# Gated mix of a state-space convolution and a shift-MLP on one core: whole first loads in another order, and the last token tile in two column pieces

## The chip, the cores and the metric

The kernel runs on one core of a Trainium2 chip. A core has a matrix engine (PE), which multiplies a stationary 128 x 128 block of weights with a moving block of up to 512 columns into a bank of PSUM; a vector engine (DVE); a scalar engine (ACT); GpSimd (POOL); and a sync engine (SP). SP and ACT also issue the transfers (DMAs) between main memory and the core's own memory. Each engine takes its instructions in program order and waits on semaphores. The metric is the device time of one execution in microseconds; lower is better.

## What is computed

Cut from the reference (one sequence of 2048 tokens with 448 channels, 1792 hidden channels):

```python
x = A_u
g = sigmoid((x * gate_w).sum(-1, keepdims=True))
a = A_ref(x, ...)                    # diagonal state-space convolution over the tokens, plus x * D_skip
h = gelu(layernorm(x) @ w1)          # 448 x 448
hs = concat([h0 shifted +1, h1 shifted -1, h2 shifted +2, h3 shifted -2]) @ w2   # four groups of 112 channels
x1 = x + hs
b = x1 + gelu(layernorm(x1) @ w3) @ w4    # 448 x 1792, 1792 x 448
return g * a + (1 - g) * b
```

## The kernel before

The tokens are worked in 4 blocks of 512, each block as 4 token tiles of 128. The work of PE is cut into units. A unit ("a", b, g) is the product of block b with one group g of the columns of w1, then its shift and gelu, then its part of the product with w2; a unit ("d", b, f) is the same for 128 hidden channels of w3 and w4. Each unit has a first product (`first`, L463, into a bank `p`: weights in the array, 512 tokens moving) and a second product (`second`, L583, into four banks `acc0` to `acc3`, one per token tile). The units of a block come in the group order 0, 2, 1, 3. Group 2 is smaller than the others: 64 columns of w1 instead of 128.

Full precision is kept by splitting: an operand is rounded by ACT to a high part (`xh`, `w1h`, `uh`, in a reduced float format) and DVE subtracts it from the original to get the low part (`xl`, `w1l`, `ul`). A product is then three products, high by high, high by low and low by high. For group 2 the high and the low columns stand side by side in one tile, `w1d`.

The layer norm ahead of w1 is folded into the weights and the output: PE computes the column means of a group of w1 (`col_means`, L851, and `presum_mean` for group 0, L900, with a constant `cm` of 1/448 as the stationary operand, into a bank `pm`), DVE subtracts them (`center`, L905), and the reciprocal deviation of each token is multiplied in later (rows turned by PE through `rows_of`, L362, then `rb`).

The first block is started piece by piece. The loads are issued by `first_loads` (L255): the three or four transfers that matter first are on two queues, ACT's and SP's, where each queue's transfers are issued in order. `w1r` holds w1 in four column groups, `raw` holds the transposed first block of x as a left half (`x0[:, :4*HW]`, in two transfers: contraction tiles 0 and 1, then 2 and 3) and a right half (L278), `xs` holds tokens by rows, `raw<-xb` are the later blocks of x.

While loads are under way, PE runs warm-up products (`warm_up`, L889): a constant tile of bf16 against itself into a bank that nobody reads, 512 columns each. The tile `warm` is set to zero by POOL (L286).

The order of the first block's steps is the string `ORDER` (L1057 to L1072), which `begin` (L1086) walks word by word. `w` is one warm-up; `m0` to `m3` the column means of a group; `c` centering; `h` and `l` high and low parts of w1; `wh`, `wl` the same for w2; `xha`, `xhb`, `xla`, `xlb` high and low parts of the left (a) and right (b) half of x; `sa`, `sb`, `ra` statistics of the tokens; `p1:h1a` a first product of unit 1 with high weights, contraction tile 1, left half; `s0:21` a second product of unit 0. The words fix the order on every engine, since all are recorded in this order. From unit 6 on, a loop over the units sets the order.

At the end, `last_two` (L619) does the second products of the last two units tile by tile: for each of four token tiles six products of 448 columns, then on DVE the add `xs = acc * gs + xs` (L631), then the output transfer of that tile (`done`, L575). `done` issues the transfer when both the convolution's part and the MLP's part of a tile are in; for the first three blocks this happens in the middle of the kernel, as the convolution's results come in.

Of the kernel before, what the change touches and what calls it, by code (L numbers as in the profile page):

```python
# [179 lines left out]
def mixer_and_small_steps(ctx, tc, xs, gg, okm, x, xT, xb, x0, w1, w2, w3, w4, gate, par, logdt, dskip, ident, out):  # L180
# [74 lines left out]
    def first_loads():  # L255
# [16 lines left out]
        act(xs[:, 0, :], x[0:128])  # L272
# [12 lines left out]
    def constants():  # L285
        nc.gpsimd.memset(warm[:, :TB], 0.0)  # L286
        nc.gpsimd.memset(cm[:, 0:1], 1.0 / D)
        nc.gpsimd.memset(cm[:64, 1:2], 1.0 / D)
# [286 lines left out]
    def done(b, j):  # L575
        q = NT * b + j
        parts[q] = parts.get(q, 0) + 1
        if parts[q] == 2:
            nc.sync.dma_start(out[q * 128:(q + 1) * 128], xs[:, q, :])

    ADDED = {}

    def second(n, only=None):  # L583
# [10 lines left out]
        for j, p in only or q:  # L594
            first_, last_ = s and p == 0, e and p == 2
            if only:
# [22 lines left out]
    def last_two():  # L619

        n = len(units) - 2
        for j in range(NT):
            t = slice(j * 128, (j + 1) * 128)
            for m in (n, n + 1):
                wh, wl = W4[units[m][2]]
                for p in range(3):
                    nc.tensor.matmul(ACC[j], (UL if p == 2 else UH)[m][:, t], wl if p == 1 else wh,  # L627
                                     start=False, stop=m > n and p == 2)
            q = NT * (NB - 1) + j
            r = xs[:, q, :]  # L630
            nc.vector.scalar_tensor_tensor(r, ACC[j], gs[:, q:q + 1], r, op0=OP.mult, op1=OP.add)  # L631
            done(NB - 1, j)

# [255 lines left out]
    def warm_up(m):  # L889
        for _ in range(m):  # L890
            nc.tensor.matmul(pw, warm[:, 0:128], warm[:, :TB], start=True, stop=True)  # L891

# [164 lines left out]
    ORDER = """  # L1057
    ws xha m0 xla m2 c0 sk xha xz xz c0 h0 w h0 l0 p0:h1a sa0 m1 c2 l0 h2 sa0 p0:h2a l2 p0:l0a w c1 p0:l2a
    p1:h2a sa1 p1:x1a p0:x0a ld m3 xla h1 xla p1:x0a sa1 p1:x2a sb3 p0:x1a p2:h0a,x1a p0:x2a,l1a c3 p0:l3a
    sa2 p1:h1a,h0a p2:x2a p0:h3a sb3 p2:h3a l1 p2:x0a xhb pe sb3 h3 p0:h0a p1:h3a p0:l1b p2:h1a p1:h0b xlb  # L1060
    xhb p2:h1b,l1b p1:h1b p3:x0a sa2 p3:h0b l3 p2:l3a p1:h2b p2:l0b p1:x1b p0:h0b sb3 p0:h2b wh0 xlb
    p3:l2b,x0b p0:x1b ra0 p0:l2b,x0b ra0 p2:x1b xlb p0:h1b p3:h0a,h3a ra0 xh1 p1:x2b ra0 p3:l3a p0:x2b ra0
    p0:h3b p3:h1a ra0 xh1 p1:x0b ra0 p3:h2a,l3b ra0 p1:h3b xh1 p0:l0b ra0 p3:h1b sk p0:l3b p3:l2a wl0 p3:l0a
    xh1 ra sk uf0 p3:l1a sk p2:x0b xl1 p3:x2b p2:h2b uf1 p3:h3b p2:l1a mu0 sk p4:l0 mu0 p2:h2a sk p4:h2 ad1
    hd0 p3:x2a p2:l0a,h3b p4:l3 hd0 mu0 mu1 p3:l0b rm mu1 p3:l1b hd0 p2:l2a p5:h0 hd0 p2:l3b xl1 s0:00 ba
    p2:x2b p4:h0,h3 hd0 xl1 p5:h2 bm p5:h1 hd0 xl1 p4:x0 wh2 p2:l2b p3:x1b s0:10 tl0 hd0 s0:20 wh1 p2:h0b
    tl0 p4:h1 s0:11 hd1 sb7 p3:h2b s0:12 p5:h3 wh3 mu2 p3:x1a s0:30 cp1 p5:x0 wl2 p5:x1,x2 hd2 s0:32 tl1
    s0:22 p4:l2 hd2 hd2 p4:x2 sb5 p4:l1 s1:21 sb7 cp2 mu3 s1:01 s0:31 p4:x1 tl2 s2:20 s0:02 s1:11 sb5 s0:21
    sb7 hd3 s2:10 s0:01 s1:20 sb5 cp2 hd3 s2:32 hd3 s1:00 sb7 s1:30 sb5 s2:30 ra1 cp3 wl1 s2:22,00,02 uf5
    ra1 s1:10 ra1 s3:10 ra1 cp3 s2:11 ra1 wl3 s1:31 s2:21,01 ra1 s3:20 ra1 s3:30 ra1 s2:31 ra1 s3:21 tl3 rn  # L1070
    ad5 s3:31 bn s3:00,11,01,22 mu4 s3:12,32,02 sb9 hd4 s2:12 re hd4 hd4 re cp4 mu5 cp4 sb9 tl4 hd5 re cp5
    re  # L1072
    """
# [12 lines left out]
    def begin():  # L1086
# [4 lines left out]
        hl_tiles(("a", 1))  # L1091
        warm_up(8)
        for word in ORDER.split():
# [175 lines left out]
```

## Time and profile before

| | us |
|---|---|
| median of 3 runs | 375.67 (375.15 to 375.73) |
| the profiled execution | 374.8 |
| span of that execution, first to last instruction | 372.9 |
| PE busy | 364.2 |
| DVE busy | 307.0 |
| ACT busy | 215.7 |
| POOL busy | 64.4 |
| mean granted clock of PE | 0.992 of full |

The span is what the trace covers; some 1.9 us of the execution lie around it. "PEld" in the views is the loading of weights into the array, which runs beside PE's products. The chain of waits is followed back from the last instruction, each step to what released it. In a row of the timeline the columns are start, length, engine, line, operation, output and inputs, shape, count, and in brackets the idle time before and what ended it. In a row of a table of windows they are, after the window and its length, the busy time and count of PE, PEld, DVE, ACT and POOL, then the granted clock, the share of the DMA engines that was busy, and the rate in GB/s. In a row of DMA issues they are the queue, the count, the size, and the time from issue to landing.

### The profile page before, as it was taken

What the parts mean: (1) busy time and instruction counts of PE and PEld (TensorE: products, weight loads), DVE (VectorE), ACT (ScalarE), POOL (GpSimd) and SP (SyncE); (2) the same over time, 40 slices, a digit from 0 to 9 for tenths busy, and PEclk for the clock granted to TensorE, in tenths of its full rate; (3) what the DMA queues carried; (4) which work ended last, traced back from release to release, by engine and by line L of the source; (5) the groups of instructions that cost most, each with busy time, mean ns of one, the idle gap of its engine ahead of it and who ended that gap; (6) DMA issues with size and microseconds to landing.
All of it is one profiled execution on the core that took longest, in us unless ns stands there. A gap on an engine that the chain in (4) does not pass through costs nothing.

```text
span 372.9 us, 5290 instructions
## 1 busy us (share of the span) xinstructions
PE 364.2 (98%) x1730; PEld 315.5 (85%) x1730; DVE 307.0 (82%) x565; ACT 215.7 (58%) x382; POOL 64.4 (17%) x177
## 2 busy tenths in 40 slices
PE   6999999999999999999999999999999999999994
PEld 3998888888888888888888888888888888888883
DVE  1899979787989997468789899998789999999422
ACT  2985759678493636945174674554756645445220
POOL 2000340200220000030023324224243324000000
PEclk9899999999999999999999999999999999999998
DMA  7995024635949055001743613457375611361212
GB/s 214 388 395 194 2 99 90 123 113 201 386 139 247 11 101 168 0 0 50 141 141 70 94 29 85 121 174 128 74 135 113 177 22 22 78 177 30 67 46 104
DMA packets 88175, 46.14 MB, mean 124 GB/s; under 512 B 67152, under 2 KB 82512, under 8 KB 87504
## 3 DMA queue, kind: packets, MB, share of 16 engines
q1 hardware_dynamic: 87696, 45.14, 44.3%
q10 hardware_dynamic: 448, 0.62, 0.6%
q8 instruction: 15, 0.25, 0.3%
q14 instruction: 16, 0.13, 0.1%
HBM read 34.74 MB, written 11.01 MB: 123 GB/s over the span
## 4 chain that ended last, share of the span: by engine, by line
PE 97%; DMA 2%; ACTq 0%; DVE 0%; issue 0%
PE p L480 48%; PE acc L602 45%; DMA w1r<-w_in 2%; PE acc L627 1%; PE pm L855 1%; PE misc L365 0%; DVE xs L631 0%; PE pw L891 0%; ACTq L269 0%; ACTq L267 0%; PE pe L833 0%; PE misc L723 0%
## 5 line engine op out<-in xcount | busy, mean ns | idle before, releaser
L541 ACT ACTIVATE uf<-p 128x512 f32<-128x512 f32 x56 | 33.5, 597 | 113.1 <-PE p L480 113.0
L480 PE MATMUL p<-xh,w3l 128*128 128x512 f32 x224 | 70.1, 395 | 0.0
L480 PE MATMUL p<-xh,w3h 128*128 128x512 f32 x224 | 70.0, 394 | 0.0
L746 DVE TENSOR_TENSOR_SCAN z<-z,carry 128x512 f32<-128x512 f32 x48 | 61.6, 1282 | 3.9
L602 PE MATMUL acc<-w4l,uh 128*128 128x448 f32 x216 | 56.3, 367 | 0.0
L602 PE MATMUL acc<-w4h,uh 128*128 128x448 f32 x216 | 56.0, 365 | 0.0
L602 PE MATMUL acc<-w4h,ul 128*128 128x448 f32 x216 | 55.9, 365 | 0.0
L571 DVE TENSOR_TENSOR ul<-uf,uh 128x512 fp32r<-128x512 f32 x56 | 38.2, 681 | 20.0 <-ACT uh L551 19.7
L480 PEld LDWEIGHTS p<-xh,w3l 128*128 128x128 f32 x224 | 42.1, 188 | 9.8
L480 PE MATMUL p<-xl,w3h 128*128 128x512 f32 x168 | 47.7, 392 | 0.0
L480 PEld LDWEIGHTS p<-xh,w3h 128*128 128x128 f32 x224 | 42.2, 188 | 6.6
L602 PEld LDWEIGHTS acc<-w4h,uh 128*128 128x128 f32 x216 | 40.5, 188 | 6.0
L602 PEld LDWEIGHTS acc<-w4h,ul 128*128 128x128 f32 x216 | 40.6, 188 | 3.5
L602 PEld LDWEIGHTS acc<-w4l,uh 128*128 128x128 f32 x216 | 40.6, 188 | 3.4
L741 ACT ACTIVATE z<-zs,nu 128x512 f32<-128x512 f32 x64 | 42.3, 709 | 0.0
L480 PEld LDWEIGHTS p<-xl,w3h 128*128 128x128 f32 x168 | 31.5, 188 | 7.2
L551 ACT ACTIVATE uh<-uf 128x512 fp32r<-128x512 f32 x56 | 35.4, 633 | 1.8
L740 POOL COPY z<-carry 128x1 f32<-128x1 f32 x48 | 32.5, 688 | 16.0 <-DVE zs L752 15.9
L748 POOL COPY carry<-z 128x1 f32<-128x1 f32 x48 | 13.5, 282 | 104.5 <-DVE z L746 103.2
L346 POOL TENSOR_TENSOR t<-r 128x4 f32<-128x4 f32 (+1 forms) x5 | 3.1, 626 | 118.1 <-DVE r L345 118.1
L746 DVE TENSOR_TENSOR_SCAN z<-z,carry,zero 128x512 f32<-128x512 f32 x16 | 20.0, 1248 | 0.0
L602 PE MATMUL acc<-w2h,uh 128*128 128x448 f32 x64 | 19.7, 367 | 0.0
(195 smaller groups left out, 540.2 us busy)
## 6 DMA issues: line engine op xcount, KB each, us to landing
zs<-xT_in SPq DMA_DIRECT2D x4, 1024.0 KB, 7.8
yd<-yt SPq DMA_DIRECT2D x56, 64.0 KB, 2.0
ysb<-yd SPq DMA_DIRECT2D x16, 224.0 KB, 2.7
out_dram<-xs SPq DMA_DIRECT2D x16, 224.0 KB, 2.9
raw<-xb_in SPq DMA_DIRECT2D x3, 1032.0 KB, 12.6
raw<-w_in SPq DMA_DIRECT2D x3, 1024.0 KB, 5.7
xd<-xt SPq DMA_DIRECT2D x16, 192.0 KB, 2.1
xr<-xd SPq DMA_DIRECT2D x16, 192.0 KB, 3.1
```

The costliest lines, as they stand in the source:

```text
L346: eng.tensor_mul(t, y, y)
L480: nc.tensor.matmul(p[:, t0:t1], (wl if w else wh)[:, k, :], (xl if x_ else xh)[:, k, o + t0:o + t1], start=(q == 0 and fresh), stop=stop i ...
L541: nc.scalar.activation(UF[n], P1[n], AF.Gelu_apprx_tanh)
L551: nc.scalar.activation(UH[n], UF[n], AF.Copy)
L571: nc.vector.tensor_sub(UL[n], uf, f32(UH[n]))
L602: nc.tensor.matmul(ACC[j], (UL if p == 2 else UH)[n][:, t], wl if p == 1 else wh, start=first_, stop=last_)
L627: nc.tensor.matmul(ACC[j], (UL if p == 2 else UH)[m][:, t], wl if p == 1 else wh, start=False, stop=m > n and p == 2)
L740: nc.gpsimd.tensor_copy(z4[:, m, 0:1], carry[:, k, m:m + 1])
L741: nc.scalar.activation(z4[:, m, 1:], ZS[b][:, k, :], AF.Copy, scale=nu[:, k, m:m + 1])
L746: nc.vector.tensor_tensor_scan(z, z, up, carry[:, k, m:m + 1], OP.add, OP.add)
L748: nc.gpsimd.tensor_copy(carry[:, k, m:m + 1], z[:, TB - 1:])
L855: nc.tensor.matmul(p, cm[:, c:c + 1].to_broadcast([128, 128]), W1R[g][:, k, :], start=k == 0, stop=k == 3)
```

## The change

Four things change.

The first loads. Before, group 0 of w1 and the first transfer of x were each issued in two pieces of 64 rows, one on ACT's and one on SP's queue, and group 2 of w1 came third on ACT's. Now group 2 is first on ACT's queue and group 0 second; x's left half is first and second on SP's; all in pieces of 128 rows. The rest follows in the order of before.

The warm-ups use a bf16 constant 1.0, broadcast, that exists before the kernel's own instructions start; the tile `warm` and its memset go. Six warm-ups stand ahead of the table's first word instead of eight, and six words `w` of it instead of two.

The table `ORDER` has another order of the same steps of the first block, for all engines.

The last token tile. Its bank `acc3`, with all units but the last two, is added to `xs` at the start of `last_two`. The last two units' products for that tile go to two banks of their own, of 320 and 128 columns, each with its own add and its own transfer. Also, the first block's four output transfers go in two pieces of 64 rows each.

The diff, without most of the table:

```diff
-    warm = big.tile([128, 2 * TB], mybir.dt.bfloat16, name="warm", tag="yt")
+    warm = nc.const_aps.tensor(1.0, [128, TB], mybir.dt.bfloat16)
...
-        for q, p in ((act, slice(0, 64)), (sp, slice(64, 128))):
-            q(w1r[p, :512], w1[p, :512])
-        for q, p in ((act, slice(0, 64)), (sp, slice(64, 128))):
-            q(r[p, :2 * HW], x0[p, :2 * HW])
         load_w1(act, 2)
+        sp(r[:, :2 * HW], x0[:, :2 * HW])
+        load_w1(act, 0)
         sp(r[:, 2 * HW:4 * HW], x0[:, 2 * HW:4 * HW])
         act(xs[:, 0, :], x[0:128])
         load_w1(sp, 1)
...
-        nc.gpsimd.memset(warm[:, :TB], 0.0)
...
         if parts[q] == 2:
-            nc.sync.dma_start(out[q * 128:(q + 1) * 128], xs[:, q, :])
+            for p in range(0, 128, 64 if b == 0 else 128):
+                t = slice(p, p + (64 if b == 0 else 128))
+                nc.sync.dma_start(out[q * 128 + t.start:q * 128 + t.stop], xs[t, q, :])
...
-            first_, last_ = s and p == 0, e and p == 2
+            first_, last_ = s and p == 0, (e or n == len(units) - 3 and j == NT - 1) and p == 2
...
         n = len(units) - 2
+        last = NT * NB - 1
+
+        def add(acc, q, c):
+            r = xs[:, q, c]
+            nc.vector.scalar_tensor_tensor(r, acc, gs[:, q:q + 1], r, op0=OP.mult, op1=OP.add)
+
+        add(ACC[NT - 1], last, slice(0, D))
         for j in range(NT):
             t = slice(j * 128, (j + 1) * 128)
-            for m in (n, n + 1):
-                wh, wl = W4[units[m][2]]
-                for p in range(3):
-                    nc.tensor.matmul(ACC[j], (UL if p == 2 else UH)[m][:, t], wl if p == 1 else wh,
-                                     start=False, stop=m > n and p == 2)
             q = NT * (NB - 1) + j
-            r = xs[:, q, :]
-            nc.vector.scalar_tensor_tensor(r, ACC[j], gs[:, q:q + 1], r, op0=OP.mult, op1=OP.add)
-            done(NB - 1, j)
+            for c in (slice(0, D),) if q < last else (slice(0, D - 128), slice(D - 128, D)):
+                acc = ACC[j] if q < last else ps.tile([128, c.stop - c.start], F32, name="p1", tag="p1", bufs=3)
+                for m in (n, n + 1):
+                    wh, wl = W4[units[m][2]]
+                    for p in range(3):
+                        nc.tensor.matmul(acc, (UL if p == 2 else UH)[m][:, t], (wl if p == 1 else wh)[:, c],
+                                         start=q == last and m == n and p == 0, stop=m > n and p == 2)
+                add(acc, q, c)
+                if q < last:
+                    done(NB - 1, j)
+                else:
+                    nc.sync.dma_start(out[q * 128:(q + 1) * 128, c], xs[:, q, c])
...
-            nc.tensor.matmul(pw, warm[:, 0:128], warm[:, :TB], start=True, stop=True)
+            nc.tensor.matmul(pw, warm[:, 0:128], warm, start=True, stop=True)
...
-        ws=each((presum,)), m0=each((presum_mean,)), w=each((warm_up, 1), (warm_up, 1), (warm_up, 1), (warm_up, 1)),
+        ws=each((presum,)), m0=each((presum_mean,)), w=each(*((warm_up, 1) for _ in range(6))),
...
-    ws xha m0 xla m2 c0 sk xha xz xz c0 h0 w h0 l0 p0:h1a sa0 m1 c2 l0 h2 sa0 p0:h2a l2 p0:l0a w c1 p0:l2a
+    w m2 xha ws w c2 m0 xla h2 xz xha w l2 sk sa0 xz c0 p1:h1a c0 p1:h0a,x0a h0 m1 xla h0 l0 sa0 w c1 p1:x1a
...
-        warm_up(8)
+        warm_up(6)
```

The order of instructions, at three places. First, PE at its first column means; `pm` with 64 columns is group 2, with `ws` group 0, the next `pm` group 1; `p` is a bank of a first product, with `w1d` that of group 2. Before:

```order
L891 MATMUL pw<-warm 128x512
L903 MATMUL pm<-w1r,cm 128x128 x2
L903 MATMUL pm<-ws,cm 128x128
L855 MATMUL pm<-w1r,cm 128x64 x4
L891 LDWEIGHTS warm
L891 MATMUL pw<-warm 128x512
L480 MATMUL p_175<-xh,w1h 128x256
L855 MATMUL pm<-w1r,cm 128x128 x4
```

and now:

```order
L901 MATMUL pw<-const-bfloat16-1.0 128x512
L865 MATMUL pm<-w1r,cm 128x64 x4
L901 LDWEIGHTS const-bfloat16-1.0
L901 MATMUL pw<-const-bfloat16-1.0 128x512
L913 MATMUL pm<-w1r,cm 128x128 x2
L913 MATMUL pm<-ws,cm 128x128
L901 LDWEIGHTS const-bfloat16-1.0
L901 MATMUL pw<-const-bfloat16-1.0 128x512
L477 MATMUL p_172<-xh,w1d 128x256 x2
L477 MATMUL p_172<-xl,w1d 128x256
L865 MATMUL pm<-w1r,cm 128x128 x4
```

The means of group 2 have moved ahead of those of group 0, and three products of group 2's unit stand ahead of the means of group 1, where one of unit 0 stood.

Second, ACT's first rows: its transfers, and the load of its function table. Before:

```order
L267 DMA w1r<-w_in 64x512
L269 DMA raw<-x_in 64x520
L264 DMA w1r<-w_in 128x256
L272 DMA xs<-x_in 128x448
L1089 ACT_TABLE_LOAD
```

and now:

```order
L264 DMA w1r<-w_in 128x256
L264 DMA w1r<-w_in 128x512
L270 DMA xs<-x_in 128x448
L1098 ACT_TABLE_LOAD
L1098 ACTIVATE rt<-cm 128x1
```

The transfer of 128 x 256 is group 2; it was third and is first, and group 0 (128 x 512), whose first 64 rows were first here, is second as a whole.

Third, the same engine where the second block of x (`raw`, 128x516) is copied and unit 0's bank is taken. Before:

```order
L910 ACTIVATE w2h<-w2r 128x448
L396 ACTIVATE xh<-raw 128x516 x4
L966 ACTIVATE uf<-p_175 128x512
L491 ACTIVATE uf<-p_194 64x512
L990 ACTIVATE ug<-uf 128x256
L993 ACTIVATE ug<-uf 16x255
```

and now:

```order
L920 ACTIVATE w2h<-w2r 128x448
L393 ACTIVATE xh<-raw 128x516 x4
L976 ACTIVATE uf<-p_190 128x512
L488 ACTIVATE uf<-p_172 64x512
L1000 ACTIVATE ug<-uf 128x256
L920 ACTIVATE w2h<-w2r 128x448
L1003 ACTIVATE ug<-uf 16x255
```

The rows up to the first gelu (`ug`) stand in the same order; one copy of w2 now stands ahead of the next.

More of the change, by code (lines that the diff above doesn't have):

```diff
@@ L1063, in mixer_and_small_steps @@
[L1063 to L1072, printed above, removed]
+    w m2 xha ws w c2 m0 xla h2 xz xha w l2 sk sa0 xz c0 p1:h1a c0 p1:h0a,x0a h0 m1 xla h0 l0 sa0 w c1 p1:x1a
@@ new lines, in mixer_and_small_steps @@
+    p0:h0a,x1a,l1a,h2a xla h1 w ld m3 l0 sa1 l1 p1:h2a sa2 p1:x2a c3 p0:h3a p2:h0a w p2:l2a sb3 p1:h3a h3
+    p0:x0a p2:h3a pe sb3 xhb sb3 p0:h1a,x2a,l0a xhb p0:l3a xlb p2:x1a p0:l1b,l2a p1:h0b sa2 p2:x0a p3:h2a
+    xlb p2:x2a p0:h1b p3:x2a sb3 xlb p2:l3a sa1 p1:x2b p2:l0b l3 p2:h1b p1:h2b p0:l3b,l2b p3:x2b wh0 p1:x1b
+    ra0 p3:h1b p2:x1b ra0 p2:h2b ra0 p1:h3b p2:h3b ra0 p0:h0b xh1 p1:h1b ra0 p0:x0b ra0 p2:x0b,l0a ra0
+    p1:x0b xh1 p0:l0b ra0 p2:h2a ra0 p0:x1b wl0 p0:h2b xh1 p0:h3b p2:h0b p0:x2b p3:h0a sk p2:l1a xh1 p3:l2a
@@ new lines, in mixer_and_small_steps @@
+    sk p3:x1a sk ra uf0 xl1 p3:x0a,x1b,l3b uf1 p3:h3a mu0 p2:h1a sk mu0 p2:l3b p4:l1 sk mu0 rm hd0 p2:x2b
+    p3:h0b ad1 wh2 p3:h3b p4:l0 p2:l2b p4:h1 hd0 sb7 mu1 p3:h2b,l2b hd0 p5:h3 mu1 p4:h2 hd0 p4:l2 s0:10 tl0
+    hd0 p3:h1a,l0b xl1 ba p3:l1a,x0b p2:l1b s0:00 bm s0:02 wl2 hd0 p5:h2 hd0 p5:h0 hd1 sb5 p3:l0a p5:h1
+    s0:30 wh1 tl0 s0:31 p3:l3a sb5 cp1 s0:12 mu2 p5:x0 p4:h0 sb7 s0:20 tl1 hd2 s0:22 p4:x0 s0:32 sb5 hd2
+    s0:21 hd2 p3:l1b s1:01 sb7 s0:11 cp2 p4:h3 xl1 s1:10 p4:l3 wh3 s0:01 sb5 s1:30 sb7 tl2 s1:11,20 p5:x1
@@ L1073, in mixer_and_small_steps @@
+    ra1 s2:10 mu3 s2:20,22,12 ra1 wl1 hd3 s2:32 s1:31 s2:30 ra1 s2:00 hd3 ra1 hd3 xl1 p4:x1 s2:01 s1:21 cp3
+    ra1 s2:11 ra1 s2:21 ra1 s2:31 cp2 ra1 cp3 p5:x2 tl3 p4:x2 uf5 s1:00 s3:20 ra1 wl3 s3:00 s2:02 s3:32 sb9
+    rn ad5 s3:21 bn s3:12,01,11,22 mu4 s3:31,02,10 mu5 hd4 s3:30 re hd4 hd4 re cp4 re hd5 tl4 cp4 cp5 re sb9
     """
```

4 lines of the change are left out of this document (removed).

## The prediction

> **What bounds the kernel now.** I read the page's first and fourth parts, then the chain in order of time, then the windows of the first 14 us.
>
> ```profile
> PE 364.2 (98%) x1730; PEld 315.5 (85%) x1730; DVE 307.0 (82%) x565; ACT 215.7 (58%) x382; POOL 64.4 (17%) x177
> PE 97%; DMA 2%; ACTq 0%; DVE 0%; issue 0%
> ```
>
> PE is 97% of the chain that ended last, and DMA is the only other share that counts. The chain says where:
>
> ```profile
> 1.98 5.83 DMA w1r<-w_in
> ...
> 7.84 1.62 PE pm L855 x8
> ...
> 10.25 1.63 PE pm L855 x8
> ...
> 12.82 0.89 PE pm L855 x8
> 13.71 1.66 PE p L480 x14
> ...
> 37.13 2.53 PE p L480 x11
> ...
> 357.89 2.55 PE p L480 x11
> ...
> 362.88 4.91 PE acc L627 x24
> 367.79 0.02 issue
> 367.81 0.68 DVE xs L631
> ```
>
> Columns: start, length, what. From 7.84 to 367.8 every piece is PE's. The block of 11 products takes 2.53 us at 37 and 2.55 at 358: the middle is a dense, even beat that the change leaves alone. Time can be won or lost only before 37.13, where that beat begins, and after 362.9. The only wait ahead is for 64 columns of w1 (group 2, issued at 1.98, landed at 7.81). The three groups of column means show a second loss: 8 matmuls take 1.62 us on 64 columns and 1.63 on 128, but 0.89 at 12.82. The windows say why:
>
> ```profile
> 4.00:6.00 2.00, 1.60 (x9) 1.05 (x6) 0.29 (x1) 0.57 (x2) 0.19 (x1) 1.00 0.64 158
> 6.00:8.00 2.00, 0.15 (x1) 0.16 (x2) 0.00 (x0) 0.62 (x1) 0.00 (x0) 1.00 1.00 357
> 8.00:10.00 2.00, 2.00 (x10) 1.63 (x11) 1.71 (x5) 1.34 (x5) 0.31 (x2) 0.56 1.04 386
> 10.00:12.00 2.00, 2.00 (x12) 1.95 (x12) 1.25 (x5) 2.00 (x7) 0.00 (x0) 0.58 1.01 359
> ```
>
> The last three columns are granted clock, DMA share and GB/s. PE did 0.15 us of work from 6 to 8, and the clock then fell to 0.56 and 0.58: some 3.4 us at half speed between 8 and 12. The DMA column shows a sag: 158 GB/s from 4 to 6, 357 and more after.
>
> **Part 1: the first loads and the order.** Group 2 goes from third place on ACT's queue to first, group 0 from first on both queues to second on ACT's, the left half of x0 from second on both to first on SP's. The bytes ahead of group 1 and of everything later are the same; two issues fewer stand ahead on SP and ACT together. So I price it by three later gates, each a thing on which PE must wait in either order, at the landings of before.
>
> ```profile
> 2.91 0.43 SPq L264 DMA_DIRECT2D w1r<-w_in  x1
> 4.75 0.83 SPq L264 DMA_DIRECT2D w1r<-w_in  x1
> 9.52 0.44 SPq L236 DMA_DIRECT2D raw<-xb_in  x1
> w1r<-w_in SPq DMA_DIRECT2D x1, 256.0 KB, 6.5
> raw<-xb_in SPq DMA_DIRECT2D x1, 1032.0 KB, 7.5
> 17.07 2.19 ACT L396 ACTIVATE xh<-raw 128x516 fp32r<-128x516 f32 x4
> 20.34 0.60 ACT L966 ACTIVATE uf<-p 128x512 f32<-128x512 f32 x1 [1.07 <-PE p L480]
> ```
>
> The fourth row answers for both w1 issues, each asked alone: landed 2.91 + 6.5 = 9.4 (group 1) and 4.75 + 6.5 = 11.25 (group 3).
>
> Gate 1, the means of group 1. Before, they ran at 10.25 to 11.88, late because the means of group 2, a warm-up and a product stood ahead at half clock. In the new order the means of groups 2 and 0 and three products stand ahead, whose loads are issued first, so I let these means start on their load, 9.4, at full clock: done at 9.4 + 0.9 = 10.3, or 1.58 earlier. Behind them the new order has three warm-ups for one and two products fewer: a product of 256 columns is 1.66/14 = 0.119, a warm-up of 512 twice that, so 2 x 0.23 - 2 x 0.12 = 0.22. Worth 1.36.
>
> Gate 2, the means of group 3: earliest 11.25, done at 12.14 instead of 13.71, or 1.57; one warm-up more and one product fewer behind: 1.46. From 13.71 to 37.13 the chain has no gap, so PE has no other slack there.
>
> Gate 3, ACT. It copies the second block of x at 17.07, as its load lands (9.52 + 7.5 = 17.0), until 19.26, and then waits 1.07 us for PE's first unit. If PE is earlier, that wait shrinks, and after 1.07 us ACT is the late one: its copy feeds the gelu of unit 0 and PE's second products. ACT's new order has the same rows there. So at unchanged landings the head gains the least of the three, **1.07 us**.
>
> All three gates move if landings do. Without the sag, 2 us x (371 - 158) = 426 KB more would have moved, 1.1 us at 386 GB/s. Nothing in the diff plainly ends it: two queues still ask for the same bytes from the start, only the 64-row pieces go. I take 0.3 of 0 to 1.1: head **1.4 us**, between 0 (last rival but one) and 2.2.
>
> Beside this: the memset of the warm tile goes, so the warm-ups may start before 1.31.
>
> ```profile
> 1.31 3.60 PE L891 MATMUL pw<-warm 128*128 128x512 bf16 x8 [1.31 <-POOL cm L288]
> ```
>
> Seven at 3.60/8 = 0.45 us are 3.2 us; begun by 1.31 they end by 4.5, fill a wait, and cost nothing unless group 2 lands before that. The output of the first block in halves puts four more issues of about 0.4 us on SP past the middle; PE's beat there asks nothing of them.
>
> **Part 2: the last tile.** The bank of the last tile is added early, an add of 0.68 us on DVE while PE still does the first of the four tiles: covered. Then 6 matmuls of 320 columns and 6 of 128 take the place of 6 of 448.
>
> ```profile
> 366.08 2.77 SPq L579 DMA_DIRECT2D out_dram<-xs  x3
> 366.40 0.36 PE L627 MATMUL acc<-w4h,uh 128*128 128x448 f32 x1
> 367.21 0.19 PEld L627 LDWEIGHTS acc<-w4h,ul 128*128 128x128 f32 x1
> 367.42 0.36 PE L627 MATMUL acc<-w4h,ul 128*128 128x448 f32 x1
> L907 DVE TENSOR_TENSOR w1r<-w1r,pm 128x256 f32<-128x256 f32 x3 | 1.2, 415 | 0.0
> 4.13 0.29 DVE L898 TENSOR_TENSOR ws<-w1r 128x128 f32<-128x128 f32 x1 [4.13 <-DMA w1r<-w_in]
> out_dram<-xs SPq DMA_DIRECT2D x1, 224.0 KB, 2.0
> out_dram<-xs SPq DMA_DIRECT2D x1, 224.0 KB, 2.8
> yd<-yt SPq DMA_DIRECT2D x56, 64.0 KB, 2.0
> ```
>
> One of 448 columns takes 4.91/24 = 0.205, one of 256 takes 0.119, so one of 320 takes 0.148. The first piece ends at 366.40 + 5 x 0.148 + 0.30 = 367.44; its add lasts 0.50 (between 0.415 for 256 and 0.68 for 448): 367.97. The second piece starts at 367.29. No row has 128 columns in this format. Below: half of 256, 0.06. Above: a weight load's 0.19. I take 0.11, the means' 0.89/8, the nearest row in columns. Then PE ends at 368.1, the add of 0.29 at 368.42 instead of 368.49. The gain is 0.07; with 0.06 it is 0.2, with 0.19 a loss of 0.4. SP issues the first piece at 368.0, 0.33 each by the last row of three (368.85 - 368.52), so it is free for the second.
>
> Landing: the last transfer of 224 KB took 2.8, the one before 2.0, so 0.8 of it is not size; 64 KB elsewhere took 2.0. The two pieces send the same bytes over the same engines 0.4 us apart, so I take 2.6 of 2.0 to 2.8. Tail: 0.07 + 0.2 = **0.27 us**, between -0.4 and +1.0.
>
> **Sum.** 1.4 + 0.27 = 1.67 us. The profiled span becomes 372.9 - 1.7 = 371.2, its execution 374.8 - 1.7 = 373.1. The median of the shown runs, 375.67, is 0.9 above that execution; I take the difference from the median: **374.0 us**.
>
> **Rivals.**
>
> *The sag goes* (chance 0.18). For it: fewer, whole pieces. Against: queues and bytes are the same. Head 2.2, tail 0.4: 373.0.
>
> *A half-speed stretch all the same* (0.15). PE may be idle twice, before the means of group 0 and of group 1. If 8 to 11 is granted half, the means of group 1 take 1.63, and products and warm-ups up to those of group 3 double: the latter end 0.6 later, 1.46 becomes 0.86, and with the tail 1.1: 374.6. [...]
>
> *Slower* (0.12): group 0 comes too late. PE takes its means in order ahead of nearly all products. Group 0 now stands second on ACT's queue. First, it had landed by 4.13, as DVE's add shows; third there, a load landed at 9.0:
>
> ```profile
> 2.62 0.44 ACTq L272 DMA_DIRECT2D xs<-x_in  x1
> xs<-x_in ACTq DMA_DIRECT2D x1, 224.0 KB, 6.4
> ```
>
> If it lands at L and the clock is half, its means take about 1.0, a warm-up 0.43, three products 0.6, the means of group 1 1.63: done at L + 3.7, plus the 0.22 of gate 1. Against 11.88 that breaks even at L = 8.0. At 9.0 the head loses 1.05, the whole 0.8: 376.5. Against it: the loads that now stand ahead of its landing (groups 2 and 0, the first of x0's left half) were the first to land before too, all by 7.81, which is just under 8.0.
>
> *The head's gain is hidden* (0.10): DVE, 1.71 us of 2 busy from 8 to 10, or the right half of x0 is the late one, and PE starts early only to wait later. Only the tail is left: 375.4.
>
> **How the numbers follow.** The forecast has 0.45. What a measurement tells from no change is 0.2%, 0.75 us: 374.9 and 376.4. Faster: 0.40 of the forecast, 0.18, and 0.09 of the half-speed case, 0.67. Same: the rest of these, 0.11, and the hidden case, 0.10: 0.21. Slower: 0.12. The range goes from 372.7 (head 2.2, tail 0.8) to 376.2, short of most of the slow case; the forecast's own is 373.3 to 374.8 (landings 0 to 0.9 earlier with the tail's smaller ends).
>
> **What would show it.** Right: the means of group 2 begin by 4 or 5 and no longer wait for the last load; means of group 1 done by 10.3 and of group 3 by 12.2; the beat that began at 37.13 begins at about 35.7; ACT's copy of unit 0 no longer waits for PE; the last add ends near 367.0. Wrong: a wait for group 0 beyond 8, clock under 0.7 around 8 to 12, a new wait on PE between 14 and 36, or a second piece whose matmuls stand 0.19 apart.

## The result: 373.17 us, faster by 0.7%

| | before | changed |
|---|---|---|
| median, 11 runs each | 375.33 (374.14 to 377.69) | 373.17 (372.26 to 374.36) |
| profiled execution / its span | 374.8 / 372.9 | 373.1 / 371.3 |

The ratio is 0.9932, 95% interval 0.9914 to 0.995: a gain of 2.6 us (1.9 to 3.2) of 375.33. The medians differ by 2.2 and the two profiled executions by 1.7 (spans 1.6). The forecast was 374.0 and 1.67. The three measures of one gain disagree because one execution of either kernel differs from the next by about as much as the change is worth (spans of the changed kernel run from 370.5 to 372.6); why is taken up below.

The chain of waits of the changed kernel, in order of time (start, length, what):

```profile
0.73 3.69 DMA w1r<-w_in
4.42 0.14 issue
4.55 1.94 PE pm L865 x8
6.49 0.43 PE pw L901
...
6.92 1.65 PE pm L913 x6
8.57 0.43 PE pw L901
9.00 0.64 PE p L477 x3
9.64 1.08 PE pm L865 x8
10.72 0.22 PE pw L901
...
11.78 0.89 PE pm L865 x8
12.67 1.18 PE p L477 x8
...
36.43 2.52 PE p L477 x11
...
362.15 3.68 PE acc L636 x18
365.82 1.51 PE p L636 x12
```

The wait for the first group of w1 now ends at 4.42 instead of 7.80, and from 4.55 on the chain is PE alone. The means of group 1 are done at 10.72 (before 11.88), those of group 3 at 12.67 (13.71). The even beat of 11 products begins at 36.43 instead of 37.13, 0.70 earlier. The last 24 products start at 362.15 instead of 362.88, so the middle takes 325.72 against 325.75 and is unchanged. From there to the end of the span it is 9.2 instead of 10.05. So the profiled pair has 0.7 in the head and 0.9 in the tail, where 1.4 and 0.27 were forecast.

PE began the means of group 2 3.3 us earlier, and its beat came only 0.7 earlier. Part of that is the order: before, the means of group 0 were done by 5.6, while PE waited for group 2; now they stand behind. The rest is the clock, as the same rows show: the 8 means of group 2 take 1.94, a warm-up 0.43, the means of group 0 1.65. These are durations at half speed; the later groups of 8 at full speed take 0.89 and a warm-up 0.22. Full speed comes within the means of group 1 (9.64, 1.08). The windows of the changed kernel (busy time of PE, PEld, DVE, ACT and POOL, granted clock, DMA share, GB/s):

```profile
4.00:6.00 2.00, 1.45 (x7) 1.48 (x8) 0.00 (x0) 0.64 (x1) 0.00 (x0) 1.00 0.91 267
6.00:8.00 2.00, 2.00 (x9) 1.41 (x9) 1.10 (x3) 0.44 (x2) 0.19 (x1) 1.00 1.04 394
8.00:10.00 2.00, 2.00 (x10) 1.78 (x10) 1.86 (x6) 2.00 (x6) 0.33 (x2) 1.00 1.06 406
```

The clock column says 1.00 from the start although the durations halve only near 9.9: it knows a clock only from the first change that the trace recorded, here at 9.9. Ahead of that, durations must be read. The last column shows the other half: 267 GB/s from 4 to 6 us, where the kernel before had 158. The sag is gone, and all landings moved. For groups 1 and 3 of w1, SP's issues in the changed kernel and, behind them, the time from each issue to its landing:

```profile
1.65 0.43 SPq L264 DMA_DIRECT2D w1r<-w_in  x1
4.43 0.33 SPq L264 DMA_DIRECT2D w1r<-w_in  x1
...
w1r<-w_in SPq DMA_DIRECT2D x1, 256.0 KB, 6.4
...
w1r<-w_in SPq DMA_DIRECT2D x1, 256.0 KB, 5.5
```

Group 1 landed at 1.65 + 6.4 = 8.1 instead of 9.4, group 3 at 4.43 + 5.5 = 9.9 instead of 11.25: 1.3 earlier. The two do it in different ways. Before, SP took 0.59, 0.83 and 0.61 us to issue the three pieces ahead of group 1; now it takes 0.40 and 0.42 for two. So group 1 was issued at 1.65 instead of 2.91, and by these rows that is all of its gain, for from issue to landing it took 6.4, much as before (6.5). Group 3 was issued only 0.3 earlier, but took 5.5 instead of 6.5.

The tail, from the timeline of the changed kernel (PE, DVE, SP's queue) and, behind it, the row of its last DMA issue (KB, us from issue to landing):

```profile
365.66 0.30 PE L636 MATMUL p<-w4h,uh 128*128 128x320 f32 x1
365.80 0.31 PE L636 MATMUL p<-w4l,uh 128*128 128x320 f32 x1
...
366.93 0.28 PE L636 MATMUL p<-w4l,uh 128*128 128x128 f32 x1
367.05 0.28 PE L636 MATMUL p<-w4h,ul 128*128 128x128 f32 x1
...
366.74 0.97 DVE L625 SCALAR_TENSOR_TENSOR xs<-p,gs,xs 128x320 f32<-128x320 f32 x2 [0.19 <-PE p L636]
...
367.32 0.85 SPq L642 DMA_DIRECT2D out_dram<-xs  x2
```

```profile
out_dram<-xs SPq DMA_DIRECT2D x1, 64.0 KB, 2.2
```

Products of 320 columns stand 0.145 apart on average, those of 128 0.11. The last add ends at 367.71, 5.56 after the start of the last 24 products; before it was 5.61. The last transfer, issued at 367.74, landed 2.2 later instead of 2.8, and the span ended 1.4 after that landing instead of 1.6.

### The profile page after: what moved, and what is told of

The parts are those of the page before. It is cut to its first block, busy times and chain, and to the rows that moved or that the text cites. A ratio compares the mean times of both kernels' runs of the same rounds, so it can differ in the third digit from the quotient of the medians.

```text
span 371.3 us, 5308 instructions
## 1 busy us (share of the span) xinstructions
PE 365.9 (99%) x1737; PEld 316.7 (85%) x1738; DVE 307.7 (83%) x567; ACT 215.7 (58%) x382; POOL 64.7 (17%) x176
## 4 chain that ended last, share of the span: by engine, by line
PE 98%; DMA 1%; DVE 0%; issue 0%
PE p L477 49%; PE acc L601 45%; PE pm L865 1%; DMA w1r<-w_in 1%; PE acc L636 1%; PE misc L362 0%; PE pm L913 0%; PE p L636 0%; PE pw L901 0%; DVE xs L625 0%; PE pe L843 0%; PE misc L733 0%
## 5 line engine op out<-in xcount | busy, mean ns | idle before, releaser
L750 POOL COPY z<-carry 128x1 f32<-128x1 f32 x48 | 33.7, 714 | 16.0 <-DVE zs L762 15.9
L601 PE MATMUL acc<-w2l,uh 128*128 128x448 f32 x64 | 19.7, 369 | 0.0
```

What stands on the lines that cost most here:

```text
L601: nc.tensor.matmul(ACC[j], (UL if p == 2 else UH)[n][:, t], wl if p == 1 else wh, start=first_, stop=last_)
L750: nc.gpsimd.tensor_copy(z4[:, m, 0:1], carry[:, k, m:m + 1])
```

## The experiments

They ran on three chips: 1 to 4, 5 to 8 and 9 to 12. The kernel before ran beside them on each (medians 376.23, 376.36 and 376.99). "Full from" is where the granted clock, or the durations, reach full speed for good.

**1. The new last tile alone** (e1_tail): the kernel before with the new `last_two`, the early add and its stop flag.

```
-            first_, last_ = s and p == 0, e and p == 2
+            first_, last_ = s and p == 0, (e or n == len(units) - 3 and j == NT - 1) and p == 2
...
+            for c in (slice(0, D),) if q < last else (slice(0, D - 128), slice(D - 128, D)):
```

> The kernel before, with the new last token tile alone (two pieces, early add), and nothing else of the change. Theory: the tail is worth what the two profiles show from the first of the last 24 products to the end, 10.05 us before and 9.15 after: 0.9 us less, of which some 0.2 hang on where the last transfer's semaphore stands in SP's closing list and may be missing here, so 0.6 to 0.9 us faster than before. Rival (the prediction's size): 0.27. Second rival: the last landing was late by chance in the one profile, and the tail is worth 0.1 or less. The first products should stay as before (beat from about 37.1).

Measured: 375.2, ratio 0.9976 (0.9955 to 0.9997), so 0.9 us with an interval of 0.1 to 1.7. The tail is worth more than 0.27, though the interval takes that in.

**2. Everything but the new last tile** (e2_head): the changed kernel with the old `last_two`.

```
-            first_, last_ = s and p == 0, (e or n == len(units) - 3 and j == NT - 1) and p == 2
+            first_, last_ = s and p == 0, e and p == 2
...
-        add(ACC[NT - 1], last, slice(0, D))
```

> The changed kernel with the old last tile (four tiles of 448 columns, one add and one transfer each). Theory: all but the tail's 0.6 to 0.9 us stays: 1.5 to 2.0 us faster than before. Rival: head and tail do not add, because an earlier head only brings the same waits later: under 0.8 faster. In the profile the beat of 11 products should begin near 36.4, as in the changed kernel.

Measured: 374.81, ratio 0.9965 (0.9949 to 0.9981), so 1.3 us (0.7 to 1.9). This is less than the theory's 1.5 to 2.0, though the interval takes that in; it is the forecast's 1.4, and not the 0.70 of the profiled pair. Yet in its own profiled execution PE reaches full speed only at 11.9, and the beat begins at 37.16, where 36.4 was expected, and later than the 37.13 of the kernel before.

**3. Whole outputs of the first block** (e3_nohalves).

```
-            for p in range(0, 128, 64 if b == 0 else 128):
-                t = slice(p, p + (64 if b == 0 else 128))
-                nc.sync.dma_start(out[q * 128 + t.start:q * 128 + t.stop], xs[t, q, :])
+            nc.sync.dma_start(out[q * 128:(q + 1) * 128], xs[:, q, :])
```

> The changed kernel, with the first block's four output transfers whole again: four transfers fewer in the middle. Theory: transfers take their eight semaphores in turn, so the last transfer's semaphore moves four places ahead in the list that SP waits for at the end; four more waits of about 0.07 us stand behind the last landing: 0.2 to 0.3 us longer from last landing to end (1.38 to about 1.65), hardly to be seen in the time. Rival: SP's four issues fewer, of 0.4 each, are worth something in the middle: faster than the changed kernel by 0.5 or more.

Measured: 373.74, ratio 0.9928 (0.9901 to 0.9955). The time does not tell it from the changed kernel. In the traces, the time from the last landing to the end of the span is 1.69 here, and 1.41 in seven of the eight profiles that have both the halves and the new tail (the eighth, experiment 6, has 1.85). The transfers take their semaphores in turn (in the two profiles of the pair eight semaphores, one after the other, for 213 and 216 transfers), so four more of them shift which one the last transfer gets. Over all fourteen profiles the stretch goes by that semaphore, as the trace numbers them: 1.85 us with 102 (experiment 6), 1.77 with 103, 1.69 with 104 (experiments 3 and 9), 1.62 with 105 (the kernel before), 1.54 with 106 (experiment 1), 1.48 with 108 and 1.41 with 110, or 0.06 to 0.08 less from each to the next. So it follows from how many transfers the program has. That SP waits for the semaphores one after the other as it closes the program is inferred from the trace.

**4. Eight warm-ups for six** (e4_warm8).

```
-        warm_up(6)
+        warm_up(8)
```

> The changed kernel with eight warm-up products at the start for six (nine with the table's first one). Theory: in its profile PE stands idle from 3.9 to 4.5, and PE runs at half speed until 9.9: 8 column means of group 2 take 1.94 us, the 6 of group 0 take 1.65. With nine warm-ups of 0.43 PE is busy without a gap from 0.77 to 4.65, and full speed may come one window (3.4 us) earlier: the column means of group 0 then in about 0.7 to 0.9, those of group 1 done by 9.5 for 10.7; up to 1 us faster than the changed kernel, if the loads then leave PE work. Rival: when full speed comes is a matter of phase and not of the gap; then 0.2 us slower, since group 2 waits for the warm-ups.

Measured: 373.07, ratio 0.9913 (0.9891 to 0.9935); full from 5.1; means of group 1 done at 10.29, of group 3 at 12.24, beat at 36.00. The seven warm-ups of the changed kernel last 3.15 us, nine last 4.0. This profile and that of experiment 2 have the same phase of the clock against the program (changes at 5.13 and 11.92 are 2 x 3.41 apart, less 0.04): with the gap filled PE is granted full speed at 5.1, without at 11.9, and the beat begins 1.16 earlier, though group 0 landed 0.37 later. The theory's grant came, but the means of group 1 were done at 10.29 and not by 9.5: PE now waited for group 0, which landed at 7.13. The time does not tell this kernel from the changed one.

**5. The old order of work with the new loads** (e5_oldorder).

```
-    w m2 xha ws w c2 m0 xla h2 xz xha w l2 sk sa0 xz c0 p1:h1a c0 p1:h0a,x0a h0 m1 xla h0 l0 sa0 w c1 p1:x1a
+    ws xha m0 xla m2 c0 sk xha xz xz c0 h0 w h0 l0 p0:h1a sa0 m1 c2 l0 h2 sa0 p0:h2a l2 p0:l0a w c1 p0:l2a
...
```

> The changed kernel with the order of work of the kernel before (new loads, new tail kept). Theory A (loads and order belong together): the old order takes the means of group 0 first, and group 0 now lands second, at about 6.9 instead of 4.1; PE begins at 6.9, 2.4 us later than the change, and the beat of 11 products that began at 36.43 begins at 37.0 to 37.6; only the tail is left, ratio 0.995 to 0.998. Rival B (the earlier landings of groups 1 and 3 are what pays, whatever the order): beat at 36.2 to 36.7, ratio 0.992 to 0.9945.

Measured: 374.58, ratio 0.9951 (0.9933 to 0.9969): the low end of theory A, and 1.8 us where the tail alone gave 0.9. The profiled execution was the slowest of its seven (span 373.4, median 372.7): PE stood idle from the end of its six warm-ups at 3.5 to 7.18, it was at half speed until 13.7, the beat began at 38.44, 0.8 later than A allowed. Neither theory is settled by it; B's early beat is not seen.

**6. The old loads with the new order of work** (e6_oldloads).

```
-        load_w1(act, 2)
-        sp(r[:, :2 * HW], x0[:, :2 * HW])
-        load_w1(act, 0)
+        for q, p in ((act, slice(0, 64)), (sp, slice(64, 128))):
+            q(w1r[p, :512], w1[p, :512])
+        for q, p in ((act, slice(0, 64)), (sp, slice(64, 128))):
+            q(r[p, :2 * HW], x0[p, :2 * HW])
+        load_w1(act, 2)
```

> The changed kernel with the split first loads of the kernel before (new order, new tail kept). Theory A: the means of group 2 come first but group 2 lands third, at 7.8; PE starts on them there with nothing done before, where the kernel before had the means of group 0 done; beat at 37.3 to 38.3, the sag of 158 GB/s from 4 to 6 us is back, groups 1 and 3 land at 9.4 and 11.2; ratio 0.996 to 1.0. Rival B (order of the work alone pays): beat at 36.2 to 36.7, ratio 0.992 to 0.9945.

Measured: 377.59, ratio 1.003 (1.0014 to 1.0046): worse than the range of theory A, and slower than the kernel before even with the new tail in it. A window and the chain of its profiled execution, one of its faster ones (376.4):

```profile
4.00:6.00 2.00, 0.00 (x0) 0.00 (x0) 0.29 (x1) 0.58 (x2) 0.00 (x0) 1.00 0.70 162
```

```profile
1.98 6.15 DMA w1r<-w_in
...
8.27 1.94 PE pm L867 x8
...
39.55 2.52 PE p L479 x11
```

The sag is back at 162 GB/s; PE has nothing to do until group 2 lands at 8.13, then works at half speed to 13.2; the beat begins at 39.55, later than A's 37.3 to 38.3. Theory B, that the order of work alone pays, has fallen.

**7. The kernel before with whole first loads, its own order of groups and of work, its own tail** (e7_whole).

```
-        for q, p in ((act, slice(0, 64)), (sp, slice(64, 128))):
-            q(w1r[p, :512], w1[p, :512])
-        for q, p in ((act, slice(0, 64)), (sp, slice(64, 128))):
-            q(r[p, :2 * HW], x0[p, :2 * HW])
+        load_w1(act, 0)
+        sp(r[:, :2 * HW], x0[:, :2 * HW])
```

> The kernel before with its first loads whole and in its own order (group 0 first on ACT's queue, the left half of x0 first on SP's, group 2 second on ACT's); order of work and tail as before. Theory A (the sag comes from the 64-row pieces): 4 to 6 us moves over 240 GB/s, groups 1 and 3 land at about 8.1 and 9.9, group 2 by about 6.9 instead of 7.8, beat 0.4 to 1.3 earlier than 37.13, ratio 0.9965 to 0.999. Rival B (the sag is chance or comes from the order of the groups): 4 to 6 us stays under 200 GB/s, landings within 0.3 of 9.4 and 11.2, ratio 0.999 to 1.001.

Measured: 374.29, ratio 0.9941 (0.992 to 0.9961): 2.2 us, more than either theory gave. From 4 to 6 us it moved 211 GB/s, between the two theories' bounds:

```profile
4.00:6.00 2.00, 2.00 (x9) 1.25 (x6) 0.99 (x2) 0.64 (x1) 0.00 (x0) 1.00 0.91 211
```

Group 1 landed at 8.11 and group 3 at 10.41, group 2 at 7.33 where A had 6.9. The spans of its 12 executions run from 370.7 to 374.6, and the profiled one (374.5) is the second slowest: in it PE is at full speed only from 13.8, and the beat begins at 37.90, 0.8 later than in the kernel before, where A had it 0.4 to 1.3 earlier.

**8. Without the six warm-ups inside the order** (e8_nowarm).

```
-    w m2 xha ws w c2 m0 xla h2 xz xha w l2 sk sa0 xz c0 p1:h1a c0 p1:h0a,x0a h0 m1 xla h0 l0 sa0 w c1 p1:x1a
+    m2 xha ws c2 m0 xla h2 xz xha l2 sk sa0 xz c0 p1:h1a c0 p1:h0a,x0a h0 m1 xla h0 l0 sa0 c1 p1:x1a
...
```

> The changed kernel without the six warm-up matmuls in its order of work (the six ahead of it stay). Theory A (PE at half speed is the bound to 9.9, so each warm-up of 0.22 to 0.43 behind a busy PE is work on the path): means of group 3 are done at 11.8 to 12.4 instead of 12.67, beat at 35.7 to 36.3, ratio 0.990 to 0.9925. Rival B (the warm-ups buy the clock): half speed lasts one stretch of 3.4 us longer, to about 13.3, beat at 36.5 to 37.8, ratio 0.993 to 0.9965.

Measured: 373.73, ratio 0.9933 (0.9911 to 0.9955), as the whole change. Full from 11.2, beat at 36.84. Neither A's gain nor B's half-speed stretch to 13.3 shows, and in the times those six neither cost nor buy anything that can be measured. One pair of profiles says more. In this one and in that of experiment 12 the clock changes on nearly the same grid (11.19 and 4.29 are 2 x 3.41 apart, and 0.07 more). The windows ahead of 4.3, this kernel's first:

```profile
0.95:4.36 3.41, 2.54 (x6) 0.59 (x4) 0.00 (x0) 1.62 (x3) 0.54 (x9) 1.00 0.67 175
```

```profile
0.88:4.29 3.41, 3.04 (x7) 0.74 (x6) 0.00 (x0) 1.49 (x2) 0.59 (x9) 1.00 0.63 186
```

With the seventh warm-up PE was at full speed from 4.3, without it from 11.2. So here the first `w` of the order did buy the clock; one pair does not say how often.

**9. Experiment 7 with the new last tile** (e9_whole_tail): the edits of experiments 7 and 1 together.

> The kernel before with whole first loads in its own order of groups and with the new last tile; its order of work, the warm tile with its memset and the whole outputs stay. Theory A (whole pieces and the tail are two independent gains, 0.0059 and 0.0024 of the time): ratio 0.990 to 0.993, spans of single executions spread over 2 us or more, since this order leaves PE idle before group 2. Rival B (the 64-channel unit first and the new order of work are needed for the gain, the run of whole loads alone was lucky in the phase of the clock): ratio 0.994 to 0.997.

Measured: 373.13, ratio 0.9893 (0.9877 to 0.991), a little better than A's range. On the same chip the changed kernel had 373.17 (experiment 12). So the two parts add, at the least, and the 64-channel unit first, with the new order of work, the constant warm tile and the halves, adds nothing that can be told beyond whole loads and the new tail. In its profiled execution PE is at full speed from 6.9, and the beat begins at 34.91, earlier than in any profile of the new order.

**10. Eight warm-ups ahead, the last four inside the order left out** (e10_warm8_few).

```
-        warm_up(6)
+        warm_up(8)
...
-    w m2 xha ws w c2 m0 xla h2 xz xha w l2 sk sa0 xz c0 p1:h1a c0 p1:h0a,x0a h0 m1 xla h0 l0 sa0 w c1 p1:x1a
+    w m2 xha ws w c2 m0 xla h2 xz xha l2 sk sa0 xz c0 p1:h1a c0 p1:h0a,x0a h0 m1 xla h0 l0 sa0 c1 p1:x1a
...
```

> The changed kernel with eight warm-ups ahead of its order of work for six, and without the last four of the six inside it. Theory A (the clock was the bound of the head; once it is full from 5 us on, the late warm-ups are work on the path, 0.22 us each): beat of 11 products at 35.1 to 35.8 against 36.00 with eight and all six, ratio 0.989 to 0.991. Rival B (without them a clock window falls under about 2 us of work and the next is granted half): beat at 36.3 to 37.5, ratio 0.992 to 0.995.

Measured: 373.19, ratio 0.9894 (0.9878 to 0.9911): A's range. But the profiled execution, the slowest of six, did what B said: half speed from 9.0 to 12.4, beat at 36.82.

**11. Three warm-ups more before the means of group 0** (e11_fill).

```
-    w m2 xha ws w c2 m0 xla h2 xz xha l2 sk sa0 xz c0 p1:h1a c0 p1:h0a,x0a h0 m1 xla h0 l0 sa0 c1 p1:x1a
+    w m2 xha ws w c2 w w w m0 xla h2 xz xha l2 sk sa0 xz c0 p1:h1a c0 p1:h0a,x0a h0 m1 xla h0 l0 sa0 c1 p1:x1a
```

> As the run before it, with three warm-ups more in PE's idle stretch of 0.9 us before the means of group 0. Theory A (a window of 3.4 us with too little work costs the half-speed stretch): no execution has one, spans agree within 1 us, ratio 0.988 to 0.991, beat at 35.1 to 35.8. Rival B (three more warm-ups only delay the means of group 0): beat 0.2 to 0.5 later than in the run before it, ratio up by 0.0005 to 0.0015.

Measured: 372.67 over 4 runs, ratio 0.9893 (0.9876 to 0.9909). The lowest median of all, but its interval and that of the changed kernel on the same chip (0.9883 to 0.9927) overlap, and its spans still run from 370.1 to 371.8, beyond A's 1 us. Full from 4.3, beat at 35.58. No version is shown to beat the changed kernel.

**12. The changed kernel again** (e12_after), with no edit.

> The changed kernel as it is, in another launch. Theory A (the phase of a free-running clock window of 3.41 us against the start of the program decides when PE is granted full speed): the profiled execution has its first full clock at another moment than 9.91, the beat of 11 products lies anywhere from 35.8 to 37.2, the spans of single executions spread over 1.5 us or more; ratio 0.991 to 0.995. Rival B (the start of the program fixes the clock): first full clock within 0.2 of 9.91, beat within 0.2 of 36.43, spans within 0.8 us.

Measured: 373.17, ratio 0.9905 (0.9883 to 0.9927), spans 370.1 to 372.6. This profiled execution has full speed from 4.3, and its timeline and chain read:

```profile
4.35 1.07 PE L865 MATMUL pm<-w1r,cm 128*128 128x64 f32 x8 [0.44 <-DMA w1r<-w_in]
6.36 0.71 PE L913 MATMUL pm<-w1r,cm 128*128 128x128 f32 x4 [0.72 <-DMA w1r<-w_in]
7.97 0.50 PE L477 MATMUL p<-xh,w1d 128*128 128x256 f32 x2 [0.45 <-DVE w1d L923]
```

```profile
1.16 5.16 DMA w1r<-w_in
...
6.34 0.04 DVE ws L908
...
7.49 0.43 DVE w1d L923
...
7.97 0.62 PE p L477 x3
8.58 0.89 PE pm L865 x8
...
10.51 0.89 PE pm L865 x8
...
35.17 2.52 PE p L477 x11
```

The same program, with groups 1 and 3 landed within 0.1 us: the means of group 1 are done at 9.47 instead of 10.72, of group 3 at 11.40 instead of 12.67, and the beat begins at 35.17 instead of 36.43, earlier even than A's 35.8. Theory A holds in its main point: the start of the program does not fix the clock (full speed for good from 9.9 in one execution, from 4.3 in the other). But the 1.26 us is not all clock. At full speed PE waited 0.72 for group 0, which landed at 6.32 here and at 6.88 in the first profile, and the chain above starts with that load. It runs over DVE: the order puts `ws`, a sum over group 0, ahead of the centering of group 2, so DVE centers group 2, whose means were done at 5.42, only after group 0 has landed at 6.32. PE's products of group 2 wait for that, and the means of group 1 start at 8.58, behind them, though group 1 had landed at 7.97. Centering ahead of `ws` was not tried.

## Where the time of one execution comes from

The profiled executions that have both the new loads and the new order, sorted by the moment from which PE is at full speed for good. The last column is the beat less the landing of group 0:

| profiled execution | group 0 landed | full from | beat begins | difference |
|---|---|---|---|---|
| 12, changed kernel | 6.32 | 4.3 | 35.17 | 28.85 |
| 11, eight ahead, five inside | 6.71 | 4.3 | 35.58 | 28.87 |
| 4, eight warm-ups | 7.13 | 5.1 | 36.00 | 28.87 |
| changed kernel, first profile | 6.88 | 9.9 | 36.43 | 29.55 |
| 3, whole outputs | 6.87 | 10.8 (full from 4.0 to 7.4 too) | 36.83 | 29.96 |
| 8, no warm-ups inside | 6.76 | 11.2 | 36.84 | 30.08 |
| 2, old tail | 6.76 | 11.9 | 37.16 | 30.40 |
| 10, eight ahead, two inside | 6.98 | 12.4 (full from 5.6 to 9.0 too) | 36.82 | 29.84 |

In the kernel before, group 2 is the late load (7.80); PE is at full speed from 4.8 to 8.3 and from 11.7, and the beat begins at 37.13.

Two things make the 2 us between these heads. Where PE is at full speed from about 5 us on, the beat follows the landing of group 0 by 28.85 to 28.87 us, and that landing differs by 0.8. Where PE is at half speed for longer, the beat comes 0.7 to 1.5 later than that. By this, 0.56 of the 1.26 us between the two profiles of the changed kernel is the landing and 0.7 the clock; that is an estimate.

The changes of the granted clock in one trace stand 3.41 us, or a multiple of it, apart (at 4.84, 8.26 and 11.67 in the kernel before), and where they fall against the start (their phase) differs from run to run: the changed kernel has one at 9.91 in its first profile and one at 4.29 in experiment 12, 5.62 apart. Windows cut at these changes, first of the kernel before, then of experiments 10, 4 and 12:

```profile
4.84:8.26 3.41, 1.17 (x11) 0.98 (x9) 0.21 (x1) 0.64 (x1) 0.19 (x1) 1.00 0.85 292
8.26:11.67 3.41, 3.41 (x18) 3.04 (x16) 2.67 (x7) 2.99 (x9) 0.31 (x2) 0.50 1.03 375
```

```profile
5.57:8.99 3.41, 2.05 (x15) 1.52 (x15) 1.99 (x6) 1.33 (x4) 0.79 (x3) 1.00 1.04 390
8.99:12.40 3.41, 3.41 (x19) 3.41 (x18) 2.18 (x6) 2.02 (x8) 0.00 (x0) 0.50 1.06 397
```

```profile
5.13:8.54 3.41, 2.28 (x16) 1.56 (x15) 1.39 (x4) 0.78 (x3) 0.57 (x3) 1.00 1.02 376
8.54:11.96 3.41, 3.18 (x25) 3.07 (x26) 3.10 (x9) 2.94 (x9) 0.22 (x1) 1.00 1.05 394
```

```profile
4.29:7.70 3.41, 2.44 (x16) 1.75 (x16) 1.36 (x4) 1.34 (x3) 0.54 (x3) 1.00 0.99 321
7.70:11.11 3.41, 3.15 (x25) 3.04 (x26) 3.11 (x9) 2.94 (x9) 0.25 (x1) 1.00 1.05 405
```

After a window with 1.17 or 2.05 us of PE work (34 and 60% of it) the next was granted half; after 2.28 or 2.44 it stayed full. Which window holds an idle stretch of about 1 us, whole or split over two, is a matter of phase, but of the landings too: experiments 7 and 9 have the same head and nearly the same phase, and PE was at full speed for good from 13.8 in one and from 6.9 in the other, where group 2 had landed 0.35 earlier.

This also settles how the profiled pair misled. The span of the profiled execution of the kernel before, 372.9, is shorter than any of the 57 taken beside the experiments (373.0 at best, medians 374.4, 374.5 and 375.2 on the three chips), and of the 11 executions beside the changed kernel one took less than its 374.8; the first one of the changed kernel, 371.3, lies in the middle of its 11 (370.5 to 372.6). A favourable execution was subtracted from an ordinary one. How much of the favour was the clock is not known; the last transfer alone, 2.6 to 3.4 us from issue to landing in three profiles of the old tail, can move a span by 0.8.

## Why the prediction was right, step by step

*What bounds the kernel: right.* PE's chain from first loads to last add, with an untouched middle.

*Landings unchanged but for 0.3 of the sag: wrong in size.* That step argued that two queues ask for the same bytes, "only the 64-row pieces go", and took 0.3 us of 0 to 1.1. It was 1.3, all of the sag and a little more. The other term of that step, the "two issues fewer", was put at nothing; by the rows above it is group 1's whole gain: fewer and shorter issues sent it off 1.26 earlier. Whole pieces alone brought group 1 to 8.11 and 8.05 (experiments 7 and 9; 8.07 in the changed kernel) and group 3 to 10.41 and 10.15 (9.95). So for the landings the pieces are most of it, and the order of the groups the rest. For the rate from 4 to 6 us each has about half: 158, 194 and 162 GB/s with the pieces (kernel before, experiments 1 and 6), 211 and 217 without them where group 0 stays first (experiments 7 and 9), and 251 to 278 with group 2 first (the changed kernel and all the others). Why less is moved while transfers are in two pieces of 64 rows is open; pieces on one queue, or whole loads with the bytes of a row changed, weren't tried.

*Gates 1 and 2, "start on their load, 9.4, at full clock": both halves failed.* In the first profile these means were done at 10.72 and 12.67 and not at 10.3 and 12.14, with loads that had landed 1.3 earlier than assumed: PE at half speed was the late one. In experiment 12 PE was at full speed and they were done at 9.47 and 11.40, earlier than forecast, but even there the means of group 1 started at 8.58, 0.6 after their load: the gate was group 0, by way of DVE, which the three gates don't have. The rival of a half-speed stretch, given 0.15, came about in part: PE was at half speed until 9.9 in the first profile, and ten of the fourteen profiles have PE at half speed at some time after 7 us.

*Gate 3, the least of the three, 1.07 us: not the limit.* ACT's copy of the second block of x was taken as fixed by its landing at 17.0. The load moved too, to 15.65, and in all three profiles the copy starts as ACT's copy of w2 ahead of it ends; so the copy moves with ACT's earlier work. In the changed kernel it started at 16.95 and the wait for PE shrank from 1.07 to 0.17; in experiment 12 (the second fence) it started at 15.70 with a wait of 0.19:

```profile
16.95 2.19 ACT L393 ACTIVATE xh<-raw 128x516 fp32r<-128x516 f32 x4
19.31 0.60 ACT L976 ACTIVATE uf<-p 128x512 f32<-128x512 f32 x1 [0.17 <-PE p L477]
```

```profile
15.70 2.19 ACT L393 ACTIVATE xh<-raw 128x516 fp32r<-128x516 f32 x4
18.08 0.60 ACT L976 ACTIVATE uf<-p 128x512 f32<-128x512 f32 x1 [0.19 <-PE p L477]
```

*Head 1.4 us: right over many executions, by two errors of opposite sign.* Loads 1.0 earlier than allowed for, clock often at half where full was assumed, and group 0 as a gate that the sum left out; experiment 2 measured 1.3 (0.7 to 1.9). That the number came out is luck. By the prediction's own signs the head of the profiled pair was wrong in part: the beat began at 36.43 and not at about 35.7, and PE at half speed until 9.9 stood among the signs of being wrong.

*Tail 0.27: too small.* Products and adds were right: 0.145 and 0.11 apart where 0.148 and 0.11 were taken, a gain of 0.05 where 0.07 stood. The landing was the mis-sized term: 2.6 was taken, 2.2 measured, 0.6 less than before and not 0.2. A last transfer of 224 KB took 2.8, 2.6 and 3.4 (kernel before, experiments 2 and 7); one of 64 KB took 1.8 to 2.35 in all eleven profiles that have the new tail. The sum had no term for what follows the last landing, which gave 0.2 more; that part goes by the count of transfers (experiment 3), and the new tail alone has 0.08 of it (1.54 in experiment 1). Together 0.9, which is also what experiment 1 measured over many runs. A single profile is no measure of it: from the first of the last 24 products to the end it is 9.7 to 10.8 in the three profiles with the old tail and 8.85 to 9.7 in the eleven with the new. One cause of that spread stands against "so it is free for the second": in experiments 4 and 10 SP took about 0.75 us to issue the first piece instead of 0.34, and the second went out 0.4 late.

*Group 0 comes too late (slower): did not happen.* Group 0 landed at 6.3 to 7.1 in the eight profiles of the table, ahead of the break-even of 8.0. But it is the next limit: with PE at full speed the beat moves with it.

*The sag goes, 373.0: this is what happened to the loads*, and the median of 373.17 stands nearer to it than to the forecast of 374.0; but its sum of 2.2 + 0.4 is not how the time was made up.

## What to carry to other kernels

Judge an edit of the head by many executions: one profile shows one phase of the clock and one set of landings, together worth 2 us here. Where PE must wait for its first loads, more warm-ups may bring full speed earlier, as in two pairs of profiles: from 5.1 and not 11.9 with 3.36 and not 2.83 us of PE work in the 3.41 us before 5.1 (experiments 4 and 2), from 4.3 and not 11.2 with 3.04 and not 2.54 in the 3.41 us before 4.3 (12 and 8); no gain of them stands in the medians here. In a fixed order of work, look on every engine for a step that needs a late load and stands ahead of one that doesn't. A first load was better issued whole: cutting two of them into 64-row halves over two queues cost 2.2 us (experiment 7), and another order of the groups and of the work won nothing on top that could be told. At the end, price the last transfer by its size (2.6 to 3.4 us for 224 KB, 1.8 to 2.35 for 64 KB here) and by what still follows its landing (1.41 to 1.85).

## What was not expected of the hardware

The granted-clock column reads 1.00 until the first recorded change, though the products ahead of it run at half speed (1.94 us for the 8 means of group 2 against 1.07 in another execution of the same kernel). PE counted as fully busy for a whole window and was still not granted full speed: in experiment 2, PE was busy for all of 5.1 to 8.5 with column means of 64 and 128 columns and two warm-ups, and full speed came one window later, at 11.9; in experiment 5, behind a window with 2.72 us of warm-ups of 512 columns, full speed was granted from 3.5 to 6.9, in which PE had nothing to do. Their windows:

```profile
5.10:8.51 3.41, 3.41 (x16) 2.66 (x15) 1.59 (x5) 1.07 (x3) 0.20 (x1) 1.00 1.04 378
```

```profile
0.08:3.49 3.41, 2.72 (x6) 0.72 (x6) 0.00 (x0) 1.34 (x2) 0.90 (x15) 1.00 0.45 115
```

By these two the busy time that the profile shows does not decide the grant alone; what does was not tried.
